# Half of the w_in transfers on a second queue, idle matrix products in more gaps, an early flag read and new transfer figures, in a kernel ordered by its own planner

## The chip, the core and the metric

The kernel runs on one core of one Trainium2 chip. The core has a matrix engine (PE, with its weight loads shown apart as PEld), a vector engine (DVE), a scalar engine (ACT), GpSimd (POOL) and a synchronisation engine (SP). SP, ACT and POOL can begin transfers (DMAs). Each engine takes its own instructions strictly in the order of the program and waits for the others through semaphores. The metric is device microseconds from start to end of one execution. All arithmetic here is float32; each matrix product that is not a transposition shows up in the records as two matmul records, so "x6" in a view of the trace can be three products of the code.

## The reference

A recurrence over 768 time steps for 4 batches and 8 heads of width 48, and then a dense block on its output:

```
for t in range(S):
    cur = einsum('bhd,bhe->bhde', u[None] * kt, vt)
    y[:, :, t] = einsum('bhd,bhde->bhe', rt, state + cur)
    state = w[None, :, :, None] * state + einsum('bhd,bhe->bhde', kt, vt)
...
h = x @ w_in                # x: 3072 x 384, w_in: 384 x 2048
g = h - np.tanh(h)
out = g @ w_out             # w_out: 2048 x 384
```

The two weights come as float64, so the kernel reads them as pairs of 32-bit words and rebuilds float32 numbers on DVE and ACT.

## The kernel before

**Units.** The recurrence is cut into 24 units: 64 time steps of two batches each. A unit loads r, k and v (two transfers of 96 KB each on SP, L605), turns r and k round on PE (`turn`, L615, matmuls at L617), scales them (L621, L625 or L629), makes the scores inside its 64 steps (`levels`, L660, and for the first four units `own_levels`, L648), masks them into the tile `at` (L752, L743), and forms its output and its state increment (`outputs`, L675, and `to_state`, L689, both through the helper at L575). The output leaves PSUM through ACT (L699 to L703); from block 1 on a part of it passes through the tile `rest`, from where POOL moves it into place with six small transfers (`fill`, L715, L717).

**Blocks and dense tiles.** Two units make a block of 256 rows (12 blocks). A dense tile is one block times 256 columns of w_in: `h` (L158), 2 x 3 products; five ACT steps (L168) and four DVE steps (L183) for h - tanh(h), which use a polynomial where |h| is small; `o` (L196), 4 products into two accumulators, `tile 0` being the first of them. There are 96 tiles. The first six blocks go through the weights in four passes of 512 columns (`PASSES`, L37), so that they can begin while only a part of the weights is there; the other six go through all of them at once.

**Weights.** A piece (L96) is 256 columns of w_in or 256 rows of w_out, 768 KB. Pieces are numbered by n: 0 and 1 are of w_in, 2 and 3 of w_out, 4 and 5 of w_in again, and so on to 15. A w_in piece comes in four transfers: two wide ones (48 partitions, 288 KB) and two narrow ones (16 partitions, 96 KB). A w_out piece is one transfer. All are begun on SP (L119) into one of four staging buffers (L116), and each piece is converted in seven steps, five on DVE and two on ACT (L133 to L139).

**The planner.** Nothing of this is issued in the order of the code. Each step is a task with an engine, a cost and the tasks that it comes after (`Plan.add`, L246). `order` (L359) runs the tasks forward and backward, tries 600 random changes of their due times with a fixed seed, and keeps the shortest plan; every engine's instruction order is that plan's. A transfer's `data` (L560, L608) is the time that it takes up of the shared transfer channel in the plan, and `lanes` allows eight transfers under way for each queue. `filled` (L385) then puts idle products (L516: the identity times itself) into gaps that the plan leaves on PE, up to the task `fill_until`, the first product `h` of tile 0 (L783); they keep the matrix engine's clock up. Their result goes to a PSUM tile that is then used for something else.

**The flag.** The kernel is built for decay factors between 0.5 and 2. DVE compares (L537) and writes a flag; after the last store, L1099 reads the flag into a register on all five engines and L1101 branches past `anywhere`, a slower path for other factors.

Of the kernel before, what the change touches and what calls it, by code (L numbers as in the profile page):

```python
# [14 lines left out]
I64 = mybir.dt.int64  # L15
# [67 lines left out]
class Weights:  # L83
# [25 lines left out]
            parts += [(d.HEAD[i], main), (slice(i * PAD + d.D, (i + 1) * PAD), rest)]  # L109
        return self.w_in_sb[:, of], parts  # L110

    def load(self, n, queue):

        dst, parts = self.piece(n)
        if self.sources[n % 4 > 1].dtype == I64:
            self.staged[n] = st = self.stage.tile([128, self.COLS], I64, name="st", tag="st", bufs=4)  # L116
            dst = st.rearrange("p (k f) -> p k f", k=dst.shape[1])
        for to, src in parts:
            yield queue.dma_start(out=dst[to], in_=src)  # L119

    def convert(self, n):

# [108 lines left out]
class Plan:  # L231
# [9 lines left out]
    BEGIN = {"PE": 1.5, "DVE": 2.2, "ACT": 1.2, "POOL": 4.3, "SP": 1.2}  # L241

    def __init__(self):
        self.tasks, self.fill, self.fill_until = [], None, None

    def add(self, engine, cost, run, after=(), due=1e9, data=0, gated=False, steps=0):  # L246
        t = SimpleNamespace(engine=engine, cost=cost, run=run, after=[x for x in after if x], due=due, data=data,
# [17 lines left out]
    def forward(self, due):  # L265

        ready = [due[t.n] - self.EARLY if t.gated else 0.0 for t in self.tasks]
        count = [len(t.after) for t in self.tasks]
        waiting = self.queues(ready, count)
        free, lanes, channel = dict(self.BEGIN), {}, 0.0  # L270
        step, bound, comes, filling = 0, self.CHUNK_0, 0.0, self.fill is not None
        starts, done, last, first, changed = [0.0] * len(ready), [], 0.0, {}, set(waiting)
        while len(done) < len(ready):
            for e in changed:
                ts = waiting[e]
                first.pop(e, None)
                if not ts:
                    continue
                start = max(free.get(e, 0.0), min(ready[x.n] for x in ts))
                t = min((x for x in ts if ready[x.n] <= start + 1e-9), key=lambda x: (due[x.n], x.n))  # L280
                if t.data:
                    start = max(start, lanes.setdefault(e, [0.0] * self.LANES)[0])
                else:

                    soon = [x for x in ts if ready[x.n] < start + t.cost and due[x.n] < due[t.n] - self.SPARE]
                    if soon:
                        t = min(soon, key=lambda x: (ready[x.n], x.n))
                        start = max(start, ready[t.n])
                first[e] = start, t
            e = min(first, key=lambda x: (first[x][0], x))  # L290
            start, t = first[e]
            waiting[e].remove(t)
            changed = {e}
            end = start + t.cost
            if e == "PE":
                if filling:
                    step += 4 * int((start - free[e]) / self.fill_cost(start))
                    filling = t is not self.fill_until
                step += t.steps
                if step >= bound:  # L300
                    each = t.cost / max(t.steps, 1)
                    crossed = end - (step - bound) * each
                    late = max(0.0, comes - crossed)
                    end += late
                    comes = max(crossed + late + self.ASKED * each + .3, channel) + self.COMES
                    bound += self.CHUNK
            free[e] = end
            if t.data:
                channel = max(channel, start + 1.2) + t.data
                end = max(end + self.LANDS, channel + self.LANDED) + self.slow(start)  # L310
                lanes[e] = lanes[e][1:] + [end]
            starts[t.n] = start
            last = max(last, end)
            done.append(t)
            for x in t.then:
                ready[x.n] = max(ready[x.n], end + self.hop(t, x))
                count[x.n] -= 1
                if not count[x.n]:
                    waiting[x.engine].append(x)
                    changed.add(x.engine)  # L320
        return last, starts, done
# [2 lines left out]

        return self.SLOW[1] if start > self.SLOW[0] else 0.0

    def fill_cost(self, start):
        return self.fill[1] * (2 if start < self.WARM else 1)

    def backward(self, plan):  # L330

# [27 lines left out]
    def order(self, tries=600):  # L359
# [20 lines left out]
            if other[0] <= plan[0]:  # L380
                plan, due = other, moved
        self.due = due
        return self.filled(plan)

    def filled(self, plan):  # L385
        _, starts, done = plan
        free, order = self.BEGIN[self.fill[0]], []
        for t in done:
            t.start = starts[t.n]
            if t.engine == self.fill[0] and free is not None:  # L390
                order += [SimpleNamespace(engine=t.engine, cost=0.0, start=free, run=self.fill[2])] * int((t.start - free) / self.fill_cost(t.start))
                free = None if t is self.fill_until else t.start + t.cost
            order.append(t)
        return order

# [18 lines left out]
def near(ctx, tc, r, k, v, w, u, out, shared, weights):  # L414


    nc = tc.nc
# [95 lines left out]
            T.transpose(tab[:, p * 128 : (p + 1) * 128], twice[:, p].rearrange("d z n -> d (z n)"), ident)  # L513


    plan.fill = "PE", .25, lambda: T.matmul(idle, ident, ident, start=True, stop=True)  # L516

    now = [add(e, 1.25 if e == "ACT" else .87, lambda e=e, at=at, x=x: e_of[e].dma_start(out=rows[at : at + NP, :, :D], in_=x.rearrange("(p i) d -> p i d", i=2)), due=-1, data=.05)
           for e, at, x in (("SP", 0, w), ("ACT", NP, u))]
# [35 lines left out]

    loads, converted = [], []
    for n in range(weights.count):
        step = steps(lambda n=n: weights.load(n, Q))
        free = converted[n - 4] if n >= 4 else None
        of = [add("SP", .55, step, [free], data=(3.3 if n % 4 > 1 else 4.0) / len(weights.piece(n)[1]), gated=True) for _ in weights.piece(n)[1]]  # L560
        if weights.sources[n % 4 > 1].dtype != I64:
            converted.append(of[-1])
            continue
        step = steps(lambda n=n: weights.convert(n))
        now = of + ([converted[n - 2]] if n >= 2 else [])
        for name, cost in (("DVE", .47), ("DVE", .47), ("ACT", .84), ("ACT", .84), ("DVE", .87), ("DVE", .87), ("DVE", .87)):
            now = [add(name, cost, step, now)]
        converted += now
# [10 lines left out]
    def unit(n):  # L579
# [20 lines left out]
        def fetch(name, src, after):  # L600
# [4 lines left out]
                Q.dma_start(out=(t.kt if to is None else to)[HALF[z], :, :D],  # L605
                            in_=src[half * 2 + z, :, steps_at, :].rearrange("h t d -> t h d"))

            of = [add("SP", .65, lambda z=z: run(z), after, data=.64) for z in range(2)]  # L608
            return add("none", 0, lambda: None, of)

        x.r = fetch("r", r, [b3.turn, b3.rk, b1.r])
# [159 lines left out]
    def hidden(j, fs, f, due, pace):  # L771
# [8 lines left out]
        x.h = add("PE", 1.29, lambda: dense.h(t, 1), [now], due + 1.3, steps=12)  # L780
        last_h[j] = x.h
        if m == 0:
            plan.fill_until = now  # L783
        x.s = add("ACT", .48, lambda: dense.act(t, "s"), [x.h, b2.c1, b2.q, b2.small, b1.s])
        x.th = add("ACT", .48, lambda: dense.act(t, "th"), [x.h, b2.g, b1.th])
        x.tg = add("ACT", .48, lambda: dense.act(t, "tg"), [x.h, b2.cp, b1.tg])
# [4 lines left out]
        x.c2 = add("DVE", .6, lambda: dense.vec(t, "c2"), [x.q, x.c1])  # L791
        x.cp = add("DVE", .65, lambda: dense.vec(t, "cp"), [x.c2, x.small, x.g])
        now = add("PE", 1.3, lambda: dense.o(t, 0), [x.cp, converted[piece + 2], b1.o] + b1.empty + ([units[1].cp, units[1].diag] if m == 0 else []), due + 2 * pace, steps=8)
        x.o = add("PE", 1.3, lambda: dense.o(t, 1), [now], due + 2 * pace + 1.3, steps=8)
        if not t.last:
            return
# [30 lines left out]
            now += 5.2 + (.95 if j + 2 < d.NB else 0)  # L827

    for t in plan.order():
        t.run()  # L830


# [232 lines left out]
def kernel(  # L1065
# [28 lines left out]
    with tc.tile_pool(name="stage", bufs=2) as stage:  # L1094
        weights = Weights(nc, stage, shared, moe_w_in, moe_w_out)
        with tc.manual_schedule():
            near(tc, r, k, v, w, u, out, shared, weights)

    far = nc.values_load(flag[0:1, 0:1], min_val=0, max_val=1,  # L1099
                         skip_runtime_bounds_check_because="a comparison's 0 or 1")  # L1100
    with tc.If(far > 0):  # L1101
        anywhere(tc, r, k, v, w, u, out, shared)


# [29 lines left out]
```

## Time and profile before

| | |
|---|---|
| median of 4 runs | 623.01 us (622.78 to 623.09) |
| the profiled execution | 625.54 us, of which the profile's span is 623.7 us |
| mean granted matrix clock | 0.990 |
| first product `h` of tile 0 begins | 25.96 us |
| first product `o` of tile 0 begins | 47.88 us |
| last product ends | 616.07 us |
| PE busy from 140 to 300 us | 160.00 of 160 us |

The times in a view of the trace count from the start of the span. In the lines of a stage, each engine has its busy time and its number of instructions, then come the granted clock of the matrix engine (1 is full speed), the busy share of the 16 transfer engines and the GB/s that they moved. In a timeline, each line has start, duration, engine, line of the code and operation, and in brackets the idle time before it with what ended it. "SPq" is the queue of SP, where transfers are begun.

### The profile page before, as it was taken

The page shows a single profiled execution, that of the slowest core. Times are in us where ns is not written, and L with a number is a line of the kernel's source. Part 1 is how long each engine was busy: PE and PEld are TensorE (multiplying, and loading weights), DVE is VectorE, ACT ScalarE, POOL GpSimd, SP SyncE. Part 2 cuts the span into 40 slices and gives each one's busy share as a digit, 9 for nine tenths or more (in the row PEclk, how much of TensorE's full clock was granted, in tenths as well). Part 3 has the DMA queues.
Part 4 walks back from the last instruction along what each step waited for, and adds up shares of the span by engine and source line. Part 5 has one row for each costly group of instructions (what it writes and reads, how often), then busy time and mean ns, then how long its engine had stood idle before and what let it go on. Part 6 is the DMA issues. An engine that isn't in the chain of part 4 may idle for free.

```text
span 623.7 us, 13185 instructions
## 1 busy us (share of the span) xinstructions
PE 599.7 (96%) x5291; PEld 445.1 (71%) x5291; DVE 429.9 (69%) x700; ACT 399.6 (64%) x873; POOL 60.7 (10%) x137
## 2 busy tenths in 40 slices
PE   8778999999999999999999999999999999999994
PEld 7657677677777777777767777777777776777772
DVE  6698979997798789866684575575575664554552
ACT  3467978977676567556574666576576575665551
POOL 3001111200000000001132011011010002001100
PEclk9988999999999999999999999999999999999999
DMA  7875489307342100002232031031031000000101
GB/s 129 173 160 101 81 128 213 71 5 123 111 77 60 48 1 1 1 12 54 50 73 63 15 58 26 14 58 40 0 57 29 13 15 21 14 2 6 27 0 30
DMA packets 86573, 33.67 MB, mean 54 GB/s; under 512 B 78536, under 2 KB 80680, under 8 KB 86504
## 3 DMA queue, kind: packets, MB, share of 16 engines
q1 hardware_dynamic: 82108, 27.15, 22.6%
q0 software_dynamic: 4224, 5.41, 3.7%
q8 instruction: 43, 0.70, 0.5%
q10 hardware_dynamic: 172, 0.20, 0.1%
q14 instruction: 26, 0.21, 0.1%
HBM read 26.94 MB, written 4.72 MB: 51 GB/s over the span
## 4 chain that ended last, share of the span: by engine, by line
PE 82%; issue 6%; DVE 4%; ACT 4%; DMA 2%; POOL 1%; SPq 1%; DVEq 0%; ACTq 0%; POOLq 0%
PE h L164 37%; PE o L202 37%; PE yk_ps L575 4%; PE x_ps L617 2%; PE x_ps L575 1%; POOL xt L717 1%; DMA xt<-rest 1%; SPq L605 1%; DMA rt<-in_r_dram 1%; DVE rT L621 1%; ACT kT L629 0%; DVE at L752 0%; ACT tg L177 0%; PE h L516 0%; ACT s L173 0%
## 5 line engine op out<-in xcount | busy, mean ns | idle before, releaser
L164 PE MATMUL h<-xt,w_in_sb 128*128 128x256 f32 x1152 | 282.8, 383 | 0.4 <-DVE w_in_sb L139 0.3
L202 PE MATMUL o<-w_out_sb,g 128*128 128x384 f32 x768 | 279.6, 489 | 1.9 <-DVE g L194 1.9
L164 PEld LDWEIGHTS h<-xt,w_in_sb 128*128 128x128 f32 x1152 | 216.8, 191 | 62.2 <-PE o L202 0.7
L202 PEld LDWEIGHTS o<-w_out_sb,g 128*128 128x128 f32 x768 | 143.1, 190 | 66.7 <-DVE g L194 3.9
L190 DVE SCALAR_TENSOR_TENSOR tg<-s,tg 128x512 f32<-128x512 f32 x96 | 66.0, 687 | 60.2 <-ACT tg L177 47.7
L188 DVE TENSOR_TENSOR g<-h,th 128x512 f32<-128x512 f32 x96 | 65.9, 686 | 59.3 <-ACT s L173 41.6
L173 ACT ACTIVATE s<-h 128x512 f32<-128x512 f32 x96 | 57.3, 597 | 70.9 <-PE h L164 70.3
L177 ACT ACTIVATE tg<-h 128x512 f32<-128x512 f32 x96 | 57.0, 594 | 44.5 <-PE h L164 44.4
L175 ACT ACTIVATE th<-h 128x512 f32<-128x512 f32 x96 | 57.1, 595 | 30.5 <-PE h L164 30.5
L194 DVE COPY_PREDICATED g<-small,tg 128x512 f32<-128x512 int32 x96 | 70.4, 733 | 4.7
L192 DVE SCALAR_TENSOR_TENSOR tg<-q,tg 128x512 f32<-128x512 f32 x96 | 66.0, 687 | 8.0 <-ACT q L179 4.8
L179 ACT ACTIVATE q<-s,m1b 128x512 f32<-128x512 f32 x96 | 69.4, 723 | 0.5
L181 ACT ACTIVATE small<-s,smallb 128x512 f32<-128x512 f32 x96 | 69.4, 723 | 0.4
L717 POOL DMA_DIRECT2D xt<-rest x66 | 32.3, 497 | 234.0 <-ACT rest L703 233.6
L641 ACT ACTIVATE at<-same,du 128x64 f32<-128x64 f32 x160 | 41.1, 341 | 0.2
L225 POOL DMA_DIRECT2D out_dram<-part x24 | 12.5, 527 | 202.5 <-DVE part L210 202.3
L210 DVE TENSOR_TENSOR part<-o,part 128x384 f32<-128x384 f32 x36 | 19.9, 552 | 12.6 <-PE o L202 12.4
L629 ACT COPY kT<-x_ps 128x512 f32<-128x512 f32 x22 | 12.9, 586 | 19.3 <-PE x_ps L617 14.2
L752 DVE COPY_PREDICATED at<-before,x_ps 128x512 f32<-128x512 int32 x24 | 17.4, 726 | 10.4 <-PE x_ps L575 10.4
L575 PEld LDWEIGHTS yk_ps<-at,vt 64*64 64x64 f32 x752 | 13.8, 140 | 14.0 <-DVE at L752 5.9
L621 DVE TENSOR_TENSOR rT<-x_ps,w_up 128x512 f32<-128x512 f32 x24 | 16.5, 688 | 9.1 <-ACT kT L629 5.3
L575 PE MATMUL yk_ps<-at,vt 64*64 64x64 f32 x752 | 17.1, 230 | 5.4 <-DVE at L752 3.1
(93 smaller groups left out, 416.7 us busy)
## 6 DMA issues: line engine op xcount, KB each, us to landing
st<-in_moe_w_out_dram SPq DMA_DIRECT2D x8, 768.0 KB, 9.2
rt<-in_r_dram SPq DMA_DIRECT2D x48, 96.0 KB, 3.2
vt<-in_v_dram SPq DMA_DIRECT2D x48, 96.0 KB, 3.0
st<-in_moe_w_in_dram SPq DMA_DIRECT2D x16, 288.0 KB, 5.9
kt<-in_k_dram SPq DMA_DIRECT2D x44, 96.0 KB, 3.3
out_dram<-part POOLq DMA_DIRECT2D x24, 96.0 KB, 2.2
out_dram<-o POOLq DMA_DIRECT2D x20, 96.0 KB, 2.1
st<-in_moe_w_in_dram SPq DMA_DIRECT2D x16, 96.0 KB, 5.4
```

The source lines that it names most:

```text
L164: self.nc.tensor.matmul(t.h2[:, z], self.w_in_sb[:, t.f // 2, kk, z * 128 : (z + 1) * 128], self.xts[t.j][:, kk].rearrange("p b t -> p (b ...
L173: A.activation(out, t.h, AF.Square)
L175: A.activation(out, t.h, AF.Tanh)
L177: A.activation(out, t.h, AF.Tanh, scale=G1)
L179: A.activation(out, t.s, AF.Square, bias=self.m1b)
L181: A.activation(out, t.s, AF.Relu, bias=self.smallb, scale=-1.0)
L188: V.tensor_tensor(t.g, t.h, t.th, ALU.subtract)
L190: V.scalar_tensor_tensor(t.tg, t.s, C4, t.tg, ALU.mult, ALU.mult)
L192: V.scalar_tensor_tensor(t.tg, t.q, K1, t.tg, ALU.add, ALU.mult)
L194: V.copy_predicated(t.g, t.small.bitcast(I32), t.tg)
L202: self.nc.tensor.matmul(self.outs[i], t.g2[:, z, i * C : (i + 1) * C], self.w_out_sb[:, t.f + z, :], start=t.first and z == 0, stop=t.last ...
L575: T.matmul(*args, skip_group_check=True, **how)
```

## The change

Four parts go in together.

1. The narrow transfers of every w_in piece are begun on POOL instead of SP. `load` takes the number of the transfer, and the queues of a w_in piece alternate.
2. Idle products get a second stretch: from the first `h` up to the first `o` of tile 0, after unit 1's scores are out of the PSUM bank to which these products write. The number for each gap is now computed in one function, `filled`, for the planner and for the program.
3. The flag is read into the registers when the plan passes 60 us; only the branch stays at the end.
4. The planner's figures for transfers change: a w_in piece takes 2.8 us of the channel instead of 4.0 us, a w_out piece 2.4 instead of 3.3, a load of r, k or v 0.58 instead of 0.64. Since the planner searches, the order of most instructions on all engines changes with this.

```diff
-    def load(self, n, queue):
+    def load(self, n, i, queue):
...
-        for to, src in parts:
-            yield queue.dma_start(out=dst[to], in_=src)
+        to, src = parts[i]
+        queue.dma_start(out=dst[to], in_=src)
...
                 if filling:
-                    step += 4 * int((start - free[e]) / self.fill_cost(start))
-                    filling = t is not self.fill_until
+                    step += 4 * self.filled(filling, free[e], start, starts)
+                    if t is filling[1]:
+                        filling = next(fills, None)
...
+    def filled(self, filling, free, start, starts):
+
+        after = [starts[x.n] and starts[x.n] + x.cost + self.HOP for x in filling[0]]
+        if None in after:
+            return 0
+        return max(0, int((start - max([free] + after)) / (self.fill[1] * (2 if start < self.WARM else 1))))
...
-        of = [add("SP", .55, step, [free], data=(3.3 if n % 4 > 1 else 4.0) / len(weights.piece(n)[1]), gated=True) for _ in weights.piece(n)[1]]
+        queues, data = (("SP",), (2.4,)) if n % 4 > 1 else (("SP", "POOL") * 2, (.85, .55) * 2)
+        of = [add(e, .55, lambda n=n, i=i, e=e: weights.load(n, i, e_of[e]), [converted[n - 4] if n >= 4 else None],
+                  data=x, gated=True) for i, (e, x) in enumerate(zip(queues, data))]
...
-            of = [add("SP", .65, lambda z=z: run(z), after, data=.64) for z in range(2)]
+            of = [add("SP", .65, lambda z=z: run(z), after, data=.58) for z in range(2)]
...
         if m == 0:
-            plan.fill_until = now
+            plan.fills.append(([], now, idle))
...
+        if m == 0:
+            plan.fills.append(([units[1].cp, units[1].diag], now, x_banks[1][:, 0, :128]))
...
     for t in plan.order():
+        if t.start > 60 and "far" not in shared:
+
+            shared["far"] = nc.values_load(shared["flag"][0:1, 0:1], min_val=0, max_val=1,
+                                           skip_runtime_bounds_check_because="a comparison's 0 or 1")
         t.run()
...
-    far = nc.values_load(flag[0:1, 0:1], min_val=0, max_val=1,
-                         skip_runtime_bounds_check_because="a comparison's 0 or 1")
-    with tc.If(far > 0):
+    with tc.If(shared["far"] > 0):
```

## The prediction

> **What bounds the kernel now.** I read the page first: span, busy row of PE, the slices.
>
> ```profile
> span 623.7 us, 13185 instructions
> PE 599.7 (96%) x5291; PEld 445.1 (71%) x5291; DVE 429.9 (69%) x700; ACT 399.6 (64%) x873; POOL 60.7 (10%) x137
> ...
> PE   8778999999999999999999999999999999999994
> DVE  6698979997798789866684575575575664554552
> ...
> PEclk9988999999999999999999999999999999999999
> DMA  7875489307342100002232031031031000000101
> ```
>
> PE is full from the fifth slice to the last but one. So time can only be won before about 60 us, in the last slice, or by sending less through PE. Second, the busy time by stage, for the early part:
>
> ```profile
> 20.00:25.00 5.00, 4.48 (x154) 3.84 (x158) 4.29 (x7) 2.32 (x7) 0.27 (x1) 1.00 1.04 181
> 25.00:30.00 5.00, 3.32 (x87) 2.52 (x80) 2.94 (x5) 2.05 (x3) 0.00 (x0) 1.00 0.83 185
> 30.00:35.00 5.00, 4.85 (x89) 3.76 (x81) 4.48 (x7) 2.23 (x4) 0.00 (x0) 0.66 0.85 241
> 40.00:45.00 5.00, 2.23 (x120) 2.10 (x123) 4.96 (x9) 3.91 (x9) 0.00 (x0) 0.93 0.73 129
> 45.00:50.00 5.00, 5.00 (x67) 4.11 (x62) 3.57 (x8) 2.82 (x11) 0.48 (x1) 0.73 0.62 109
> 60.00:70.00 10.00, 9.90 (x221) 7.58 (x215) 9.59 (x19) 9.87 (x31) 2.88 (x6) 1.00 0.47 87
> ```
>
> The first busy figure is PE, the third DVE, the fourth ACT; then come the clock and the transfer share. Between 25 and 60 us PE idles some 8 us and runs three spells at half clock (one lies in 30:35, one across 40:50, one in 54 to 58). DVE is the fuller engine there, and before 30 us the transfer engines are. Third, the timeline around the two gates:
>
> ```profile
> 15.90 0.56 DVE L133 TENSOR_SCALAR power<-st 128x768 uint32<-128x768 uint32 x1 [0.51 <-DMA vt<-in_v_dram]
> 17.43 0.57 PE L575 MATMUL x_ps<-rT,kT 48*64 48x64 f32 x23 [1.65 <-issue]
> 17.93 2.05 PE L516 MATMUL h<-ident 128*128 128x128 f32 x16
> 20.68 0.73 DVE L752 COPY_PREDICATED at<-before,x_ps 128x512 f32<-128x512 int32 x1 [3.28 <-PE x_ps L575]
> 26.06 0.56 DVE L133 TENSOR_SCALAR power<-st 128x768 uint32<-128x768 uint32 x1 [0.24 <-DMA st<-in_moe_w_in_dram]
> 30.16 2.52 PE L164 MATMUL h<-xt,w_in_sb 128*128 128x256 f32 x6
> 44.39 1.13 PE L575 MATMUL yk_ps<-at,vt 64*64 64x64 f32 x32 [2.18 <-DVE at L743]
> 47.88 2.75 PE L202 MATMUL o<-w_out_sb,g 128*128 128x384 f32 x8
> ```
>
> DVE stands still for 3.28 us while PE waits for instructions (1.65) and then runs eight idle products (16 records, 2.05) ahead of unit 1's own scores. Half of the first `h` takes 2.52 us at half clock; the chain of waits has it at 1.29 later.
>
> **Parts 1 and 4: queue and order.** I go by the instruction order of the built program, with the distances of before's rows (start to start: L133 and L134 0.48 us, L137 to L139 0.88, mask L752 0.63, scaling L621 0.61). The order now has DVE begin both w_in pieces before unit 1's masks, so three arrivals matter.
>
> Piece 0: before, three transfers begun in 1.70 us from 9.61, the last at about 10.7; converted at 15.90 after a wait: 5.2 us. Piece 1: four in 2.05 from 17.23, the last at 18.8; converted at 26.06: 7.3 us. Now SP has no narrow ones ahead: piece 0's second wide transfer goes at 9.61, so it is there between 14.8 and 16.9; I take 15.2, its place in the stream being the old one. Piece 1's last wide one follows two wide (0.57 each) and two v loads (1.31): begun at 12.06, there at 17.3 to 19.4; I take 19.0, the streams being full. Unit 2's k now stands behind w_out: 3.84 MB with everything ahead of it, against 3.58 MB moved by 25 us (five stages of 34 to 182 GB/s); at that pace 26.5, at the 241 GB/s of the stage with w_out in it some 3 us less; I take 25.0.
>
> POOL's four issues cost it 0.5 us each by the nearest rows (`xt<-rest` 497 ns with 16 partitions, `out_dram<-part` 527 with 64): 5.4 to 7.5 us. POOL next copies `extra` at 9.42, which waits for v: hidden. Later narrow issues stand among the `rest` transfers of blocks 2 and 3, two microseconds in an engine that is busy 2.88 of 10.
>
> The Trainium skill ("SBUF — State Buffer", section "SBUF: two separate sides") speaks against this part: VectorE's two-port operations keep GpSimd from writing its descriptors, and a 620 ns transfer took about 3100. Here `xt<-rest` is begun in 497 ns on the mean with DVE busy beside it; by the rule the narrow parts would be some 2.5 us late (an estimate) and still arrive with the wide ones, so the sum would be the same.
>
> Replay: DVE converts piece 0 at 15.2, scales unit 1 at 15.7 and 16.3, waits for piece 1 to 19.0, masks unit 1 from 19.95 to 21.3. Unit 1's output starts at 21.35 (before 22.57) and takes 1.35 with the state. Eleven idle products follow (ten records took 1.28, so 0.256 each, 2.8 in all) to 25.5, while DVE has 2.65 of L137 and L138, waits for k to 25.0, and finishes piece 0 at 26.5. **First `h` at 26.5, 0.5 later than before.** But piece 1 is nearly converted, which cost DVE 3 us after 26 us before. Unit 2's scaling starts at 28.55; its levels and own scores are done at 30.85, the second half of `h` at 32.15 in full clock (before 32.6); masks 31.1 to 32.45, output 32.5 (33.46); the next `h` 34.7 to 37.3 (36.47); unit 3's levels 38.05 (40.59); its masks wait for these, output 40.95 (44.39) to 42.3; two turns (0.43 each), eight idle products (2.0): **first `o` at 45.7 against 47.88, so -2.2.** Bounds: +1.0, if piece 1 and k come 3 us after my times; -4.0, if all come by the early ends.
>
> **Part 2: idle products.** 57 instead of 34. Of the 12 in the new stretch, 4 (1.0 us) lie in the wait for unit 3's masks (2.18 before) and cost nothing; the other 8 are inside the replay, as are the 11. Cover gone, all 23 are on the path: +5.9. What they buy is inside too: half clock followed stretches in which PE was busy for about half of the time (1.42 of 2.00 us at 40:42, then 0.21 of 2.00 at 42:44, and then the clock fell to 0.5). In the replay those before 30.6 and 44.3 are fuller. The third spell I leave.
>
> The skill's "TensorE: Matmul & The Clock Gate" (section "HAM oscillation — how this bites in real kernels") makes idle gaps over about 3.4 us the danger; the longest here is 2.2, yet the clock fell. By its rule the fills would win nothing; keeping, as an estimate, half of one 3.4 us spell would make -0.5 of the -2.2. The rows decide.
>
> **Part 3: flag.** At the end it stands in the way:
>
> ```profile
> L1099 PEldq TENSOR_LOAD <-flag x1: 492/492/492, 613.2 to 613.2; - x1
> L1099 ACTq TENSOR_LOAD <-flag x1: 765/765/765, 617.2 to 617.2; - x1
> L1099 SPq TENSOR_LOAD <-flag x1: 1067/1067/1067, 617.2 to 617.2; - x1
> ...
> L1101 SPq EVENT_SEMAPHORE  x8: 17/17/17, 621.5 to 622.0; - x8
> L1101 ACTq EVENT_SEMAPHORE  x1: 17/17/17, 621.3 to 621.3; - x1
> ```
>
> SP and ACT end their last issues at 617.2 and read the flag (1.07 and 0.77) before they branch; 3 us behind the branches both signal. Without the read SP is 1.1 earlier, ACT 0.75, so ACT comes last at about 620.55: **-1.0** (bounds -0.75 and -1.2; the last stores land 2.2 to 3.2 us after 616.7, just under). In the first pass the reads cost PE nothing where matmuls run meanwhile, as at 613.2; behind ACT's 0.77 stands tile 2's tanh, behind DVE's 0.69 the next unit's row sums, in a stage where both are over 95% busy and PE waits for them: +0.4, between 0 and 0.8.
>
> Later loads: pieces 4 to 7 are begun some 15 us earlier and next to other fills. PE idles 1.02 us at 110:120 behind such loads: 0, between -1.0 and +1.0.
>
> **Sum** on the profiled span: 623.7 - 2.2 - 1.0 + 0.4 = 620.9, that is -2.8. The span and the runs' median (623.0) differ by 0.7, the profiled execution (625.5) has 1.8 around the span; I take -2.8 off the median: **620.2**.
>
> **Rivals.** (a) Slower: piece 1 gates. DVE can do nothing for unit 1's masks until it has landed, and behind them stand piece 0's last steps and the first `h`. For: every load before 25 us shares full transfer engines, and its row is 26.06. Against: SP begins it 6.7 us sooner. The gain of 2.8 is gone when it lands at 21.8; at 24.0 it is 625.2. (b) Start won, then lost: at 60 to 125 us DVE (9.59 of 10) and ACT (9.87) set the pace, so an earlier first `o` meets the same wall; left are -1.0 + 0.4: 622.4. Against: PE idles 0.1 us there. (c) More: the third half-clock spell (1.7 lost) and the 1.02 idle go too: 617.5. (d) The fills do not do what they say: they overrun by half, +2.9: 623.1, within the noise.
>
> **How the numbers follow.** Forecast 0.48, its own range 618.3 to 621.8; (a) 0.20, (b) 0.12, (c) 0.12, (d) 0.08. A measurement tells 0.2% (1.25 us) from no change: faster is below 621.8. Forecast and (c) and a little of (b) make 0.64; the rest of (b), (d) 0.15; (a) and the tail of (d) 0.21. The range 616.8 to 624.6 leaves out the far ends of (a) and (c).
>
> **What would show it.** The flag's reads near 65 us and the last signals by 620.6 on the old scale; clock at full speed from 30 to 34 and 44 to 48 us; first `h` near 26.5 and first `o` near 45.7; DVE waiting for piece 1 at about 18 for no more than 2 us. Wrong, if that wait passes 4 us, if the idle products before the first `h` end after piece 0's last step, or if PE has new idle time after 60 us.

## The result and the profile after

| | before | after |
|---|---|---|
| median of all runs | 622.98 us (78 runs, 621.72 to 627.49) | 622.17 us (49 runs, 620.64 to 624.85) |
| ratio to before, 95% interval | 1 | 0.9984 [0.9978, 0.999] |
| profiled execution / its span | 625.54 / 623.7 us | 622.26 / 620.5 us |
| first `h` / first `o` of tile 0 | 25.96 / 47.88 us | 31.30 / 50.48 us |
| last copy on DVE ends | 616.65 us | 614.06 us |

The change makes the kernel 1.0 us faster (0.0016 of 623; the two medians differ by 0.8); the forecast was 2.8. The two spans differ by 3.2 us only because the first profiled execution of before was 2.5 us slower than its median. So the medians count, not the spans.

The page of the kernel after, with its slices (each digit is a fortieth of the span):

```profile
span 620.5 us, 13303 instructions
...
PE 601.3 (97%) x5337; PEld 447.1 (72%) x5337; DVE 430.0 (69%) x700; ACT 398.7 (64%) x873; POOL 68.8 (11%) x153
...
PE   7799999999999999999999999999999999999995
...
DVE  5789889998985797776676747475666555455552
...
PEclk9899999999999999999999999999999999999998
DMA  7966795244420000011233111211210100100101
```

PE has 46 more records than before, which are the 23 idle products more; POOL has the 16 narrow issues. Otherwise the picture is that of before. The stages of the start, with the same columns as those of before:

```profile
20.00:25.00 5.00, 4.51 (x78) 4.08 (x78) 1.95 (x4) 2.49 (x4) 0.27 (x1) 0.70 1.09 232
25.00:30.00 5.00, 4.20 (x102) 3.86 (x102) 5.00 (x7) 1.21 (x3) 0.00 (x0) 0.96 0.70 168
30.00:35.00 5.00, 4.84 (x118) 4.23 (x117) 4.42 (x9) 3.42 (x7) 0.00 (x0) 1.00 0.86 178
40.00:45.00 5.00, 3.90 (x113) 3.12 (x112) 4.66 (x9) 4.56 (x13) 0.00 (x0) 1.00 0.68 124
45.00:50.00 5.00, 3.95 (x88) 3.70 (x88) 4.33 (x8) 4.61 (x18) 0.93 (x2) 1.00 0.76 135
55.00:60.00 5.00, 5.00 (x120) 4.36 (x115) 4.89 (x9) 4.14 (x16) 0.00 (x0) 1.00 0.41 73
60.00:70.00 10.00, 9.88 (x236) 7.43 (x227) 9.96 (x19) 9.57 (x27) 4.18 (x9) 1.00 0.58 107
```

From 30 us on the clock is granted in full (before had 0.66 at 30 and 0.73 at 45); a spell at half clock now lies ahead of that (0.70 in 20 to 25 us, where before had 1.00). DVE, the third busy figure, does 1.95 us of work in 20 to 25 us where it did 4.29. The timeline tells what it waits for. First the four narrow transfers of pieces 0 and 1 on POOL:

```profile
5.38 2.19 POOL L120 DMA_DIRECT2D st<-in_moe_w_in_dram  x4
```

```profile
9.62 3.69 SPq L120 DMA_DIRECT2D st<-in_moe_w_in_dram  x2
...
14.10 0.63 PE L626 MATMUL x_ps<-ident,rt 128*128 128x128 f32 x4 [1.00 <-DMA rt<-in_r_dram]
...
17.01 0.56 DVE L134 TENSOR_SCALAR power<-st 128x768 uint32<-128x768 uint32 x1 [1.13 <-DMA st<-in_moe_w_in_dram]
...
20.49 0.38 PE L524 MATMUL h<-ident 128*128 128x128 f32 x1 [2.50 <-issue]
...
23.01 0.56 DVE L134 TENSOR_SCALAR power<-st 128x768 uint32<-128x768 uint32 x1 [3.31 <-DMA st<-in_moe_w_in_dram]
...
25.53 0.58 PE L584 MATMUL yk_ps<-at,vt 64*64 64x64 f32 x24
...
27.86 2.72 PE L524 MATMUL h<-ident 128*128 128x128 f32 x22
...
28.44 0.95 DVE L140 TENSOR_TENSOR w_in_sb<-w_in_sb,power 128x768 f32<-128x768 f32 x1
...
31.30 1.46 PE L165 MATMUL h<-xt,w_in_sb 128*128 128x256 f32 x6
...
50.48 1.53 PE L203 MATMUL o<-w_out_sb,g 128*128 128x384 f32 x4 [1.54 <-DVE g L195]
```

In before, r of unit 1 was turned here:

```profile
11.88 0.63 PE L617 MATMUL x_ps<-ident,rt 128*128 128x128 f32 x4 [0.33 <-DMA rt<-in_r_dram]
```

SP needs 3.69 us for two issues; r of unit 1, whose transfers are begun at 6.94 as before (6.93), is turned at 14.10 (11.88 before); piece 0 is there at 17.01, piece 1 at 23.01 after a wait of 3.31. PE waits 2.50 us for nothing that the profile shows (`issue`); the prediction called such a wait one for instructions, and the last section shows why that is likely. Unit 1's output begins at 25.53. The first `h` comes 5.3 us later than in the profile of before, the first `o` 2.6 later. Yet the kernel ends sooner. The flag's reads, in the records of its line and of the branch:

```profile
L843 ACTq TENSOR_LOAD <-flag x1: 465/465/465, 65.3 to 65.3; - x1
L843 DVEq TENSOR_LOAD <-flag x1: 542/542/542, 66.5 to 66.5; - x1
...
L843 SPq TENSOR_LOAD <-flag x1: 732/732/732, 67.5 to 67.5; - x1
```

```profile
L1114 SPq EVENT_SEMAPHORE  x8: 17/17/17, 618.3 to 618.8; - x8
...
L1114 ACTq EVENT_SEMAPHORE  x1: 17/17/17, 618.6 to 618.6; - x1
```

They are short and lie at 65 to 68 us. The last copy on DVE, in before and in after:

```profile
616.09 0.56 DVE L217 COPY o<-o 128x384 f32<-128x384 f32 x1 [0.73 <-PE o L202]
```

```profile
613.50 0.56 DVE L218 COPY o<-o 128x384 f32<-128x384 f32 x1 [0.73 <-PE o L203]
```

From its end to the end of the span it is 6.5 us now, and was 7.1.

### The profile page after: what moved, and what is told of

The parts are those of the page before. It is cut to its first block, busy times and chain, and to the rows that moved or that the text cites. A ratio compares the mean times of both kernels' runs of the same rounds, so it can differ in the third digit from the quotient of the medians.

```text
span 620.5 us, 13303 instructions
## 1 busy us (share of the span) xinstructions
PE 601.3 (97%) x5337; PEld 447.1 (72%) x5337; DVE 430.0 (69%) x700; ACT 398.7 (64%) x873; POOL 68.8 (11%) x153
## 4 chain that ended last, share of the span: by engine, by line
PE 82%; DVE 5%; DMA 3%; ACT 3%; SPq 2%; issue 2%; POOL 0%; DVEq 0%; POOLq 0%; ACTq 0%
PE h L165 37%; PE o L203 36%; PE yk_ps L584 5%; PE x_ps L626 2%; SPq L614 2%; DMA rt<-in_r_dram 1%; PE x_ps L584 1%; DMA kt<-in_k_dram 1%; DVE rT L630 1%; PE h L524 1%; DVE tg L193 1%; DMA st<-in_moe_w_in_dram 1%; DVE g L195 1%; ACT kT L638 0%; DVE tg L191 0%
## 5 line engine op out<-in xcount | busy, mean ns | idle before, releaser
L189 DVE TENSOR_TENSOR g<-h,th 128x512 f32<-128x512 f32 x96 | 65.9, 687 | 50.2 <-ACT s L174 31.6
L638 ACT COPY kT<-x_ps 128x512 f32<-128x512 f32 x22 | 12.9, 587 | 20.3 <-PE x_ps L626 14.7
L584 PEld LDWEIGHTS yk_ps<-at,vt 64*64 64x64 f32 x752 | 13.1, 134 | 11.2 <-issue 4.2
L226 POOL DMA_DIRECT2D out_dram<-o x20 | 10.6, 533 | 95.7 <-ACT o L220 95.5
L584 PEld LDWEIGHTS yk_ps<-rT,state 48*64 48x64 f32 x704 | 12.3, 134 | 10.9 <-DVE state L732 4.1
```

Of the source, the lines that this page charges most:

```text
L189: V.tensor_tensor(t.g, t.h, t.th, ALU.subtract)
L584: T.matmul(*args, skip_group_check=True, **how)
```

## The experiments

A difference of 0.001 is 0.62 us. All ratios are to before, measured on the same chip beside it; where two variants are compared through their ratios, the text says whether the intervals overlap.

**1. The flag by itself.** It is the one part that can be moved without touching any plan. First a second copy of before, for the scatter:

> The kernel before, unchanged, for its noise and a second profile. The two profiles so far differ by 3.2 us in span, but the runs by 0.8 to 1.0. If the first profile of before was a slow execution (625.5 against a median of 623.0), this one's span is near 621.2 and its loss of matrix time before 130 us is smaller than the 39.1 us of the first. If the first was typical, its span is again near 623.7 and the runs hide something. Ratio 1.000.

1.0007 [0.9989, 1.0025], 623.23 us. Its profile has the first `h` at 29.09 instead of 25.96, with no edit:

```profile
18.06 0.91 PE L575 MATMUL x_ps<-rT,kT 48*64 48x64 f32 x23 [2.27 <-issue]
...
29.09 1.53 PE L164 MATMUL h<-xt,w_in_sb 128*128 128x256 f32 x6 [0.30 <-DVE w_in_sb L139]
```

The `issue` wait, 1.65 us in the profile that the prediction used, is 2.27 here. One profile of the start is one draw. Then the flag, in before:

```diff
     for t in plan.order():
+        if t.start > 60 and "far" not in shared:
+            shared["far"] = nc.values_load(...)
         t.run()
...
-    far = nc.values_load(flag[0:1, 0:1], ...)
-    with tc.If(far > 0):
+    with tc.If(shared["far"] > 0):
```

> The kernel before with only the flag read moved to 60 us of the plan; nothing else moves. Theory 1 (the tail term of the prediction is right): 0.7 to 1.0 us faster (ratio 0.9984 to 0.9989), which would be the whole gain of the change. Theory 2 (the reads in the first pass give it back, where DVE and ACT are full): no difference (0.9997 to 1.0003).

0.9988 [0.9973, 1.0004], 622.59 us. And the reverse edit in after:

> The changed kernel with the flag read at the end again, every order as it was. Theory 1: 0.7 to 1.0 us slower than the changed kernel, so equal to before (ratio 0.9995 to 1.0005), and the new order and the fills together are worth nothing. Theory 2 (the read is worth nothing): as the changed kernel, ratio 0.998 to 0.999.

1.0000 [0.9985, 1.0015], 622.94 us. With after at 0.9984 the flag is worth -0.0012 in before and -0.0016 in after, and -0.0015 in the pair of experiment 6: three pairs on plans that do not change, all of one sign, 0.75 to 1.0 us. Each pair alone has overlapping intervals. The traces settle it: from the end of the last copy on DVE to the end of the span it is 7.1 to 7.4 us in all eight profiles with the reads at the end, and 5.5 to 6.8 us in all twelve with the reads at 60 us. What remains of the change without the flag is 1.0000, with an interval of 0.9 us to either side: **the flag is the whole net gain; queues, order and idle products together are worth nothing that can be measured.**

**2. The idle products.** They are left out of the program in their place, while the plan keeps its order; no output uses them. First the 12 between the first `h` and the first `o`:

```diff
-                order += [... self.fill[0](to))] * n
+                order += [... self.fill[0](to))] * (0 if filling[0] else n)
```

> The changed kernel without the 12 idle products between the first h and the first o; every other instruction stays. Theory 1 (the fills hold the clock up, which is what catches the late start up): a spell at half clock of 3.4 us comes back between 44 and 58 us and the time rises by 0.5 to 1.7 us (ratio 0.999 to 1.001). Theory 2 (they only fill waits, the catching up is DVE's earlier conversion): no spell, time as the changed kernel or up to 0.5 us less (0.9975 to 0.9985).

1.0024 [1.0005, 1.0043], 624.22 us: 2.05 us over after in the medians, 2.5 by the ratios, whose intervals do not overlap. The half clock is back. Its stages, five microseconds each:

```profile
45.00:50.00 5.00, 3.50 (x72) 3.17 (x72) 4.20 (x8) 3.96 (x13) 0.00 (x0) 0.66 0.35 66
50.00:55.00 5.00, 3.52 (x60) 2.18 (x64) 4.50 (x8) 4.32 (x15) 2.92 (x6) 0.74 0.81 155
55.00:60.00 5.00, 5.00 (x90) 3.14 (x83) 2.84 (x5) 0.07 (x1) 0.00 (x0) 0.58 0.03 7
```

Clocks of 0.66, 0.74 and 0.58 stand where after has 1.00. Next, the 11 before the first `h` (the edit is `* (0 if n > 10 else n)`), because they overran: they end at 30.58, while piece 0's last step on DVE was done at 28.44 + 0.95 = 29.39.

> The changed kernel without the 11 idle products ahead of the first h; everything else stays. In its profile they run from 27.86 to 30.58 us, and piece 0 is converted at 29.39. Theory 1 (they overrun and the start passes through): the first h comes at about 29.5 instead of 31.3 and the time falls by 1 to 1.8 us (ratio 0.9955 to 0.997). Theory 2 (the start is caught up later whatever it is, or the lower clock takes it back): first h earlier, time within 0.5 us of the changed kernel (0.9975 to 0.9992).

0.9985 [0.997, 0.9999], 621.66 us, first `h` at 30.71, first `o` at 50.38. The overrun is real and costs nothing: what is won before the first `h` is not seen at the end, nor at the first `o`. Last, the same second stretch added to before's own order (15 products, planner untouched; the stretch begins behind unit 1's scores and ends at the first `o`):

```diff
+        plan.fill2 = [units[1].cp, units[1].diag], now, lambda: T.matmul(x_banks[1][:, 0, :128], ident, ident, ...)
...
-                free = None if t is self.fill_until else t.start + t.cost
...
+                second = second or t is self.fill_until
+                free = None if t is self.fill2[1] else t.start + t.cost
```

> The kernel before with its orders as they are and 15 idle products set into the gaps of its plan between the first h and the first o (the change's second stretch alone, without planning anew). Theory 1 (the second stretch is worth some 2 us by the clock, as its removal from the changed kernel cost): the half-clock spells near 31 and 44 to 48 us go, ratio 0.996 to 0.9985. Theory 2 (in an order not planned with them they sit on the path): same or slower, 1.000 to 1.004.

1.0000 [0.9981, 1.0019], 622.99 us. This run did to before what the forecast said of the change: first `h` at 25.66, first `o` at 44.58, 2.8 us sooner than in before_again, spells at half clock gone from 20 up to 50 us. By the medians it brought nothing, and one spell came back later (0.66 at 50 to 55 us). Part of the 2.8 us is the draw of the start: the profiled execution of before_again is 0.9 us slower than its median, that of before_fill2 lies on its own, and before_flag_early, without these products, has its first `o` at 45.75.

**3. The queue.** Did POOL's early narrow transfers push r and piece 1 back? In after_narrow_late the four of pieces 0 and 1 are held and run after unit 0's `extra` copy, at 9.84 instead of 5.38 us:

```diff
+        for t in of:
+            t.held = n < 2 and t.engine == "POOL"
...
+            x.extra.frees = n == 0
...
+        if getattr(t, "held", False):
+            held.append(t)
+            continue
         t.run()
+        if getattr(t, "frees", False):
+            for x in held:
+                x.run()
```

> The changed kernel with the four narrow transfers of pieces 0 and 1 issued on POOL behind the first copy of v's thirds (about 9.5 us) instead of at 5.5. Theory 1 (begun on their own queue they overtake the loads that SP has waiting, and this made r of unit 1 land at 14.1 instead of 11.9 and piece 1 at 23.0): r of unit 1 is there near 12, k near 13, piece 1 at 21 to 22, first h 1 to 2 us earlier than 31.3. Rival (the late arrivals come from SP's own limit of eight transfers under way and from w_out, not from the narrow ones): nothing moves by more than 0.5 us before the first h. In time: a gain of 0.5 to 1.5 us if the start passes through, none if it is caught up.

0.9975 [0.9962, 0.9989], 621.57 us, an interval that overlaps with that of after. Its timeline:

```profile
9.61 1.19 SPq L120 DMA_DIRECT2D st<-in_moe_w_in_dram  x2
...
9.84 2.18 POOL L120 DMA_DIRECT2D st<-in_moe_w_in_dram  x4 [0.36 <-issue]
...
12.94 0.60 PE L628 MATMUL x_ps<-ident,rt 128*128 128x128 f32 x4
...
21.43 0.58 PE L524 MATMUL h<-ident 128*128 128x128 f32 x1 [4.64 <-issue]
...
22.84 0.56 DVE L134 TENSOR_SCALAR power<-st 128x768 uint32<-128x768 uint32 x1 [2.61 <-DMA st<-in_moe_w_in_dram]
...
33.12 1.46 PE L165 MATMUL h<-xt,w_in_sb 128*128 128x256 f32 x6
```

The overtaking is shown: SP's two issues take 1.19 instead of 3.69, and r of unit 1 is turned 1.16 us sooner. But piece 1 is there at 22.84, as in after (23.01), although its last wide transfer is begun at 12.16 instead of 14.67: its landing does not follow the moment of its issue. That it follows the bytes ahead of it is my reading; the transfer share is 1.06 or more in every five microseconds from 10 to 25 us, in both runs. The first `h` is at 33.12, the latest of all, in a kernel that is not slower; but this profiled execution, 622.72 us, is the slowest of the kernel's twelve. And all narrow transfers back on SP, each in its place of the same plan:

```diff
-        of = [add(e, .55, lambda ...: weights.load(n, i, e_of[e]), ...
+        of = [add(e, .55, lambda ...: weights.load(n, i, Q), ...
```

> The changed kernel with all its plan and orders, but the narrow transfers begun on SP at the places that the plan gave them (four issues in a row on SP at about 5 us, ahead of piece 0's first wide one). Theory 1 (the second queue itself helps: SP is spared 16 issues and their slots): r and k of unit 1 land later than with POOL, first h after 32 us, time 0.5 to 2 us more than the changed kernel. Theory 2 (all queues share the same 16 transfer engines, so only the order of the bytes counts, and that is nearly the same): within 0.5 us of the changed kernel (ratio to before 0.9978 to 0.9992).

0.9988 [0.9975, 1.0002], 622.46 us: the same as after, with r of unit 1 turned at 14.31 and piece 1 there at 23.05. SP now begins r at 9.12, behind the narrow transfers, and r comes as late as when POOL began them. So it was the early begin of the narrow transfers, not the second queue, that delayed r. The queue from which the narrow transfers are begun is worth nothing measurable.

**4. The planner's figures.** Exchanged both ways; here the plan is searched anew, so every order moves.

```diff
-        queues, data = (("SP",), (2.4,)) if n % 4 > 1 else (("SP", "POOL") * 2, (.85, .55) * 2)
+        queues, data = (("SP",), (3.3,)) if n % 4 > 1 else (("SP", "POOL") * 2, (1.0, 1.0) * 2)
...
-            of = [... after, data=.58) ...]
+            of = [... after, data=.64) ...]
```

> The changed kernel with the planner's old figures (1.0 us of the channel for each of a w_in piece's four transfers, 3.3 for w_out, 0.64 for r, k and v); it is planned anew, so all orders change. Theory 1 (the optimistic figures put waits for weights in front of unit 1's work): DVE waits for piece 1 less than the 3.3 us of the changed kernel, first h before 29 us, time 0.5 to 2 us less. Theory 2 (any two plans of this planner differ by about a microsecond either way, whatever the figures): within 1.5 us of the changed kernel on either side, with no relation to the first h.

0.9919 [0.9895, 0.9943], 618.29 us: four microseconds faster than after (the intervals do not overlap), with the first `h` at 30.95 and the first `o` at 50.75, as late as in after. And the new figures in before:

```diff
-        of = [... data=(3.3 if n % 4 > 1 else 4.0) / ...]
+        of = [... data=(2.4 if n % 4 > 1 else 2.8) / ...]
...
-            of = [... after, data=.64) ...]
+            of = [... after, data=.58) ...]
```

> The kernel before with only the planner's new figures (2.8 us for a w_in piece over its four transfers on SP, 2.4 for w_out, 0.58 for r, k and v), planned anew. Theory 1 (the figures are too optimistic for this chip): slower than before by 0.5 to 2 us, with DVE waiting longer for pieces. Theory 2 (the figures don't matter beyond the noise of planning): within 1 us of before.

0.9915 [0.9891, 0.9939], 618.06 us: five microseconds faster than before. Old figures help the new code and new figures help the old one, so neither set is better by itself; that one suits the one code and one the other is not excluded by this pair. That asked for the planner's own scatter.

**5. Other seeds.** The search draws its 600 changes from `Random(3)`; 4 and 5 are two more draws.

```diff
-        chance = Random(3)
+        chance = Random(4)
```

> The kernel before with the planner's random seed 4 instead of 3; nothing else. Theory 1: within 0.7 us of before. Theory 2: between 618 and 626, most likely 1.5 us or more away from 622.8.

0.9953 [0.9937, 0.9969], 620.26 us.

> The changed kernel with the planner's random seed 4 instead of 3; nothing else. Theory 1 (the time is the sum of the parts of the change; a plan is as good as another): within 0.7 us of the changed kernel. Theory 2 (the luck of the search decides by microseconds, as the two kernels with exchanged figures suggest, both 4 us faster than their own): between 617 and 624, most likely 1.5 us or more away from 622.2.

1.0013 [0.9996, 1.003], 624.17 us.

> The kernel before with seed 5. Luck theory: anywhere from 618 to 625. Parts theory: as seeds 3 and 4, mean 621.5, and the changed kernel's seeds below.

0.998 [0.9958, 1.0003], 621.26 us.

> The changed kernel with seed 5. Luck theory (the plan that the search ends on moves the time by some 2 us, whatever the parts of the change): anywhere from 618 to 625, and the mean over three seeds of the changed kernel no better than that of the kernel before. Parts theory (the change is worth its 1 us on top of the luck): mean over the seeds about 1 us below that of before.

0.9964 [0.9947, 0.998], 620.28 us. Seeds 3, 4, 5 make 0.9984, 1.0013, 0.9964 of after (mean 0.9987) and 1, 0.9953, 0.998 of before (mean 0.9978). The seed alone spreads either kernel over 3 us, more than the whole change, and over three seeds the change shows no gain. With this scatter three seeds could not have shown a gain of a microsecond. The exchanged figures with seed 4:

> The kernel before with the new figures and seed 4; with seed 3 the new figures made it 4.5 us faster (618.1). If the new figures are better there (queue on SP alone), it is about 4 us below before's seed 4 (620.3), so near 616. If seed 3 was luck, anywhere from 618 to 625.

0.9977 [0.996, 0.9993], 621.27 us: 1.5 us slower than before with the same seed. For before, the gain from the new figures belongs to one seed.

> The changed kernel with the old figures and seed 4; with seed 3 the old figures made it 4 us faster (618.3). If the old figures are better (they match the packets' own mean times), it is again about 4 us below the changed kernel of the same seed (624.2), so near 620. If seed 3 was luck, anywhere from 618 to 625.

0.9961 [0.9945, 0.9977], 620.67 us: 3.3 us faster than after with the same seed, though its first `o` comes at 56.44 us. Two seeds of two favour the old figures in after; that is a hint, not shown.

**6. The parts that held, on the best plan.** before with the new figures and the early flag:

> The kernel before with the new figures (618.1 on its own) and the flag read at 60 us of the plan; the plan is the same. If the flag's worth adds to any plan: 0.7 to 1.0 us less, 617.2 (ratio 0.990). If not: 618.1 (0.9915). Either way it should beat both kernels of the study.

0.9900 [0.9874, 0.9927], 617.11 us. The same with the second stretch of idle products (18):

> The same with 18 idle products set into the plan's gaps between the first h and the first o, without planning anew. In the order of the kernel before such products were worth nothing (1.000), in the changed one taking 12 away cost 2 us. If they help wherever a half-clock spell is left (here one ends near 35 us): 0.5 to 1.5 us less than without. If they sit on the path: the same or up to 1 us more.

0.9889 [0.9867, 0.9911], 616.04 us, the lowest median of all, 6.9 us under before, from five runs; its interval overlaps with that of before_new_figures. Its page and two stages:

```profile
span 614.7 us, 13265 instructions
...
PE 599.1 (97%) x5315; PEld 445.9 (73%) x5315; DVE 429.8 (70%) x700; ACT 399.6 (65%) x873; POOL 60.2 (10%) x137
```

```profile
45.00:50.00 5.00, 4.35 (x84) 3.53 (x83) 4.79 (x9) 4.91 (x16) 3.02 (x6) 1.00 0.71 135
50.00:55.00 5.00, 5.00 (x85) 3.96 (x84) 5.00 (x9) 3.88 (x14) 0.00 (x0) 1.00 0.71 132
```

The clock is full in both; without the added products (new_figures_flag) it was 0.50 and 0.89. It is not full everywhere: from 20 to 35 us it is 0.80 to 0.86. The -0.0011 of the added products lies within the intervals. The narrow transfers stay on SP.

**Where the time lies.** To compare plans I took the elapsed time less the work that the matmuls begun by then do at full clock (records times 0.2153 us for `h`, 0.323 for `o`, 0.1075 for a turn, 0.0156 for the small ones, idle products nothing). This is a sum over the records of one profiled execution each, good to some tenths of a microsecond:

| us not used by real products up to | 30 us | 60 us | 130 us | 600 us | from 60 to 600 | profiled execution | median of runs |
|---|---|---|---|---|---|---|---|
| before | 19.7 | 32.4 | 39.3 | 49.2 | 16.9 | 625.54 | 622.98 |
| before_again | 21.1 | 30.5 | 38.0 | 47.6 | 17.1 | 624.15 | 623.23 |
| before_flag_early | 19.9 | 30.3 | 37.3 | 47.3 | 17.0 | 623.28 | 622.59 |
| before_fill2 | 18.8 | 29.0 | 36.5 | 46.2 | 17.2 | 622.95 | 622.99 |
| after | 23.3 | 31.7 | 37.5 | 47.3 | 15.6 | 622.26 | 622.17 |
| after_flag_end | 22.2 | 32.5 | 38.2 | 47.9 | 15.4 | 623.69 | 622.94 |
| after_no_fill11 | 23.1 | 31.6 | 37.3 | 47.1 | 15.5 | 621.49 | 621.66 |
| after_narrow_late | 23.3 | 32.5 | 38.2 | 47.9 | 15.4 | 622.72 | 621.57 |
| after_narrow_sp | 23.3 | 31.3 | 38.2 | 47.6 | 16.3 | 622.46 | 622.46 |
| after_no_fill2 | 23.3 | 35.8 | 41.7 | 51.4 | 15.6 | 625.74 | 624.22 |
| after_old_figures | 23.0 | 31.1 | 35.8 | 43.8 | 12.7 | 618.30 | 618.29 |
| before_new_figures | 20.1 | 27.1 | 31.8 | 40.2 | 13.1 | 615.79 | 618.06 |

Two things stand in it. Within one order, what is lost by 60 us is still lost at 600: the four profiles of before's order differ by 3.4 us at 60 us and all lose 16.9 to 17.2 behind it, those of after's order differ by 4.5 and lose 15.4 to 15.6 (16.3 with the narrow transfers on SP). So nothing of a late start is made up behind 60 us, and what sets the profiles of one order apart comes almost whole from before 60 us. Between orders, the loss from 60 to 600 us differs: 17 in before's, 15.5 in after's, 12.7 and 13.1 in the two fast plans; so a good plan wins 3 to 4 us behind the start. It is a matter of the draw: with seeds 4 and 5 this loss is 14.3 and 15.7 for before, 15.8 and 14.7 for after.

## Why the prediction was right in sign and wrong in size

The sign came out right by the flag alone. The main step, an earlier start, did not come, and that the new order gave back behind 60 us what the start lost was luck, a draw of the planner's search.

**The flag: right.** -1.0 + 0.4 was forecast, -0.75 to -1.0 measured. The tail behind the last copy is 0.6 us shorter in this pair of profiles, a little under the lower bound of 0.75; over all profiles (7.1 to 7.4 against 5.5 to 6.8) it is 1.2 shorter on the mean, the upper bound. Whether the reads in the first pass cost some of the +0.4 is within the noise of the runs.

**The start-up term: the step that failed.** "First `o` at 45.7 against 47.88, so -2.2" measured 50.48, and what all parts but the flag were to bring, -2.2, measured -0.2 to 0.0 (the change's -1.0 less the flag's -0.75 to -1.0). It fails at three points.

- *The arrivals.* "I take 19.0, the streams being full": piece 1 came at 23.01, 3.6 us past the late end of my bounds. I let its landing follow the time of its issue. That issue was itself late, at 14.67 instead of 12.06, because two issues on SP took 3.69 us; but run after_narrow_late shows that the landing does not follow it: begun 2.5 us sooner, piece 1 was there 0.17 sooner. Piece 0 came at 17.01, just outside 14.8 to 16.9.
- *What I left out.* PE's `issue` wait stood in my own fence (1.65 us) and got no term in the replay. It was 2.50 here, and 2.27, 3.80 and 4.64 in other runs. POOL's narrow transfers, begun from 5.38 us on, went ahead of r of unit 1 and made its turn 2.2 us late, 1.16 of which after_narrow_late gives back; my replay took that turn as it was. So unit 1's output started at 25.53, not 21.35, and the idle products overran as I had named as a sign of being wrong. The clock was full from 30 us on, as I had named too, but my replay had no half-clock spell at 22 us.
- *The conversion.* Even a right replay would have given a wrong time: a first `o` at 50.48 makes +2.6 by my rule, and the kernel is faster. I carried the shift of the first `o` to the end one to one. Within one order that is nearly so (the table: what is lost by 60 us stays lost). But the new order differs behind the first `o` as well. The same 19.4 us of real work stand ahead of it in both kernels; from there to 60 us before loses 3.9 us (before_again 2.5), after 0.7 and after_no_fill2 3.7, so it is the second stretch of idle products that saves this. By 60 us after has lost 0.7 less than the profile of before, with a first `o` 2.6 us later. And for what lies behind the start I put 0, between -1.0 and +1.0; the new order loses 1.5 us less from 60 to 600 us, and some 0.7 less behind them (the end of the last copy less the loss at 600 us is 567.4 to 567.7 us in before's order, 566.8 in after's). Over all plans the first `o` says nothing of the time: at 46.05 it goes with 624.17 us (after_seed4), at 50.75 with 618.29, at 56.44 with 620.67; 17.6 us of real work stand ahead of the first of these, 22.3 ahead of the last.

How much the start lost can be estimated. If each profile of the table is put at its kernel's median by taking off the distance between the two, before's order without added products has lost 29.6 to 29.8 us by 60 us, after's order with its second stretch of idle products 31.3 to 31.8: some 2 us worse instead of 2.2 better.

**Rival (a)** had its condition met: piece 1 at 23.0 us, past the break-even at 21.8, and the wait of 3.31 stayed just under the 4 us that I set. Its price, 624.2 for that landing, did not come: 622.17. The estimate of 2 us for the start and 0.75 to 1.0 for the flag come to about that price; what it lacks is the gain of the new order behind 60 us.

**Rival (b)** comes nearest to the time, 622.4, but not by its mechanism: the start was not won, and within one order the later stages take nothing away. The idle time that I held against it, 0.1 us, is that of 60 to 70 us alone; from 60 to 120 us PE idles 2.1 us in before and 1.2 in after. **Rival (c)**'s third half-clock spell did go in after, but it is missing in before_again too (1.00 from 45 to 60 us), so it was no property of the kernel to be won.

**The idle products: undersized.** I let all of them lie inside the replay. In this order the second stretch keeps 2.0 to 2.5 us, and the clock from 45 to 60 us is what differs in the two profiles. As order, queues and products net to nothing, the rest of them costs about as much. In before's order the stretch is worth nothing. Rival (d), an overrun that costs 2.9: the overrun came and cost nothing (after_no_fill11).

**POOL's issues: right.** Four narrow issues took 2.19 us, 0.55 each, and 2.18 in after_narrow_late, where DVE works beside them. The waits for descriptors that the Trainium skill ("SBUF — State Buffer", section "SBUF: two separate sides") warns of do not show in them; but the page measured them beside a plain copy on VectorE, and none ran beside these issues, so the runs do not test that case. PE has no new idle time past 60 us: 9.88 of 10 at 60 to 70, against 9.90, and from 60 to 120 us less than before.

**What stays open:** what in a plan makes it lose 3 to 4 us less between 60 and 600 us; whether the old figures are truly better in after; why the load of instructions comes later in some executions than in others. None of these was tried by itself. No more than three seeds were run, and the best version only with one.

## What to carry to other kernels

Where a planner with a random search sets the order, an edit to its costs is a new draw: measure the scatter over seeds first, and judge each part with the plan held fixed. When an order changes, do not price the start by the moment of one product alone: add up what the busiest engine has left unused by fixed times, behind the start as well, since the new order can differ there too. And here, with the transfer engines full, an earlier issue was not an earlier arrival (begun 2.5 us sooner, there 0.17 sooner).

## What the runs showed of the hardware

**The clock falls without a long gap.** In after_no_fill2, two-microsecond stages before a spell, and PE's gap in them:

```profile
42.00:44.00 2.00, 2.00 (x98) 1.58 (x96) 2.00 (x5) 2.00 (x5) 0.00 (x0) 1.00 0.83 147
44.00:46.00 2.00, 0.05 (x5) 0.05 (x4) 2.00 (x5) 1.87 (x7) 0.00 (x0) 0.88 0.75 138
46.00:48.00 2.00, 2.00 (x65) 1.91 (x66) 2.00 (x4) 1.50 (x6) 0.00 (x0) 0.50 0.32 60
```

```profile
43.36 0.65 PE L584 MATMUL x_ps<-rT,kT 48*64 48x64 f32 x32
45.95 1.13 PE L584 MATMUL yk_ps<-at,vt 64*64 64x64 f32 x32 [1.95 <-DVE at L761]
```

PE stood idle for 1.95 us, and the clock fell to 0.50 at about 45.5 us, 1.5 us into the gap (0.88 is the mean of the stage). The Trainium skill ("TensorE: Matmul & The Clock Gate", section "HAM oscillation — how this bites in real kernels") makes gaps over about 3.4 us the danger; here one of 1.95 was enough, and with the 12 idle products in place the clock stood at 1.00 through these stages.

**The `issue` wait follows a load of instructions.** This wait of PE between 16 and 22 us was 1.65 and 2.27 us in two executions of before, and 2.50, 2.97, 3.80 and 4.64 in after, after_narrow_sp, after_no_fill11 and after_narrow_late, which have one plan; the first `h` of one and the same kernel came at 25.96 and 29.09 us. The page of after lists a queue of this kind (packets, MB, share of the 16 engines):

```profile
q8 instruction: 44, 0.72, 0.5%
```

That is 16 KB a packet. The transfer records of the traces have one such packet near this place. It ends at 16.06 and 16.61 us in the two of before and at 18.54, 19.09, 20.06 and 19.59 in the other four, each time 1.4 to 2.1 us before PE goes on. In after_old_figures it ends at 15.80 us and the wait is 0.62, in after_flag_end at 14.96 and there is none. That PE waits for these instructions is my reading; the records do not name the engine that they are for.

**An issue can be slow.** Two issues on SP took 3.69 us where POOL had begun four narrow transfers before them, 1.19 us where POOL began them at the same time.
